# Attention, an MLP and a mixing layer in one fp32 kernel: PSUM banks of attention and of the first MLP part shared out anew, with some key parts, load steps and additions moved between queues

## The chip, the cores and the metric

The kernel runs on one core of a Trainium2 chip. The number that counts is device time in microseconds (us): the median of the runs of the whole program, launched once per run. Before the change it is 1717.0 us. A core has five engines that work side by side and meet through semaphores: TensorE (PE in the rows; PEld is its weight load), VectorE (DVE), ScalarE (ACT), GpSimd (POOL) and SyncE (SP), which here issues the DMAs. Each executes its own instructions strictly in the order in which they were written. PSUM, where PE puts its sums, has eight banks, and a bank can take a new sum only when the old one has been read out.

## What is computed

Three layers follow each other, all in fp32:

```python
def _attn_ref(q, k, v, w_phi):                     # 8 batches, 8 heads, 576 tokens, 64 wide, 128 features
    def phi(x):
        proj = np.einsum('bhsd,df->bhsf', x, w_phi)
        proj = proj - np.max(np.abs(proj), axis=-1, keepdims=True)
        return np.concatenate([np.exp(proj), np.exp(-proj)], axis=-1)
    q_p, k_p = (phi(q), phi(k))
    kv = np.einsum('bhsf,bhsd->bhfd', k_p, v)
    z = np.sum(k_p, axis=2)
    num = np.einsum('bhsf,bhfd->bhsd', q_p, kv)
    den = np.einsum('bhsf,bhf->bhs', q_p, z)[..., None] + 1e-06
    return num / den

def _moe_ref(x, g_ln, w_ch1, w_ch2):               # 512 -> 2048 -> 512
    mu, var = mean and variance of x over its last axis
    xn = (x - mu) / np.sqrt(var + 1e-06) * g_ln
    return x + np.maximum(xn @ w_ch1, 0.0) @ w_ch2

def _moe2_ref(x, w_theta, w_tok_r, w_tok_i, w_ch):
    theta = x @ w_theta
    y = mix over tokens of x * cos(theta) and x * sin(theta)
    u = x + y
    return u + np.maximum(u @ w_ch, 0.0)
```

## The kernel before

Each fp32 operand is split into a high and a low part, and a product is three matmuls (`mm3`, L72: high by high, high by low, low by high). So for every operand one engine rounds the high part and another subtracts it from the value to get the low part. `lo_vec` (L62) does that on DVE in one instruction, `lo_cut` (L68) on POOL in pieces.

**Attention** is cut into 16 units (a pair of batches by a pair of heads), each with five groups of token tiles. For the keys of a group (`Unit.keys`, L277) PE projects into a bank of `pj`, DVE takes the maximum `m` and subtracts it (`ys`), ACT does two exponentials (`pf`) and rounds the high part `kph`, and DVE makes the low part `kpl` in one instruction of 128x1024. Then PE adds keys times values into `kv` (`values`, L292). Queries (`queries`, L334) go the same way but are transposed by PE into the bank `tr` first; their low part `qp` is made on POOL. From groups 2 and 4 on, `numer` (L371) forms four numerators per batch, whose banks alternate between `nm` and `tr`, ACT copies each to `num`, and `norm` (L394) transposes `num` back. Units 0 to 4 keep their queries, and unit 0 its keys, in plain fp32 (`NATQ`, `NATK`), with no low parts.

**MLP A**, the first quarter of the MLP's 2048 hidden columns, is written into attention as filler at low priority, in 18 chunks of 256 tokens. `tokens` (L469) transposes two tiles through `ph`. Two up sums (`up`) follow, each of 256 hidden columns, in the one bank `ph`, and relu gives the parts `hh`, `hl`. The down sums (`down`) of both token tiles stay open in two banks of their own (`acc0`, `acc1`) from the first hidden block to the last, and `flush` (L505) runs the down sums of one block only after the next block's up sums. What attention leaves over is done behind it, with `wide` chunks that also use `pj`, `tr` and `nm`.

**MLP B** does the other three quarters in two rounds (`r`) over nine chunks of 512 tokens, with seven products in place of eight for each hidden block (`Hidden`, L712). `first()` makes `pa`, `pb`, `pc`; ACT copies `p1`, `u2`, `u3` out; `relu` makes the hidden parts `hb`; `second()` finishes the last two; `down` adds into four `acc` banks, one block later. `tokens_b` (L634) makes the sums `c1` to `c4` of a chunk on POOL and all high and low parts on ACT and DVE. Beside this, `advance` (L813) runs load steps that turn the 64-bit weights of later stages into fp32 parts (`raw`, `bits`, `val`, `mag`).

**The mixer** follows with its own banks.

The program text gives each instruction a priority, and a scheduler at build time chooses from it the order in which they stand on each engine. So an edit of the text moves instructions far away from it. `tc.high_priority(offset=...)` shifts the priority, and a negative offset makes filler. `tc.issue_after(ins)` puts what a block writes behind `ins` on the engine of `ins`.

Of the kernel before, what the change touches and what calls it, by code (L numbers as in the profile page):

```python
# [51 lines left out]
def body(ctx, tc, qT, kT, va, wbd, g, w1, w2, wth, wtok, wch, out):  # L52
# [78 lines left out]
    class Mlp:  # L131
# [32 lines left out]
        def down(self, f, acc, hh, hl):  # L164
            for j in range(2):
                wh, wl = self.w2[2 * f + j]
                for i in range(CT):
                    o = slice(i * P, (i + 1) * P)
                    mm3(acc[i], hh[:, j, o], hl[:, j, o], wh, wl, f == 0 and j == 0,
                        f == self.nf // 2 - 1 and j == 1)  # L170

        def relu(self, pool, ph):
# [14 lines left out]
    ps_pj, ps_tr, ps_kv, ps_nm, ps_ph, ps_ac = (pool("pj", 2), pool("tr", 1), pool("kv", 1), pool("nm", 1),  # L187
                                                pool("ph", 1), pool("ac", 1))
# [29 lines left out]
    class Unit:  # L218
        def __init__(self, u):
# [5 lines left out]
            self.final = FINAL and u == NPAIR * NHP - 1  # L225
            self.natk, self.natq = (u < NATK), (u < NATQ or u >= LASTQ)

# [49 lines left out]
        def keys(self, gi):  # L277
# [11 lines left out]
            lo_vec(kl[:, :2 * n], kp[:, :2 * n], kh[:, :2 * n])  # L289
# [44 lines left out]
        def queries(self, gi):  # L334
# [29 lines left out]
            for b, c0, o, m in parts:  # L364
                dh, dl = (t[:, :, :, c0:c0 + m].rearrange("p h s c -> p (h s) c") for t in self.qp[b])
                src = qv[:, :, o:o + m]
                hi_act(dh, src)
                lo_cut(dl, src, dh)
            return lambda: self.numer(gi)

        def numer(self, gi):  # L371
            if gi in (2, 4):
                b = 0 if gi == 2 else 1
                kh, kl = self.kv[b]
                for h in range(2):
                    for hf in range(2):
                        if hf:
                            nm = ps_tr.tile([D + 1, 288], F32, name="tr")
                        else:
                            nm = ps_nm.tile([D + 1, 288], F32, name="nm")  # L380
# [13 lines left out]
        def norm(self, t0):  # L394
            if self.alone & 1:
                xp = ps_ac.tile([P, 6, D + 1], F32, name=f"acc{t0 // 3 % 2}")
# [61 lines left out]
    def mlp_a(m):  # L458
# [44 lines left out]
        pend = None  # L503

        def flush():  # L505
            x, acc, f, hh, hl, ch = pend
            m.down(f, acc, hh, hl)
            if f == m.nf // 2 - 1:
                for i in range(CT):
                    V.tensor_tensor(x[i], acc[i], x[i], op=ALU.add)  # L510
                    SY.dma_start(out=xp_d[ch][:, i, :], in_=x[i])

        nxt = None
        for ch in range(NCH):
# [7 lines left out]
            acc = [ps_ac.tile([P, DM], F32, name=f"acc{i}") for i in range(CT)]  # L522
            for f in range(m.nf // 2):
# [5 lines left out]
                hh, hl = m.relu(p_ma, ph)  # L529
# [4 lines left out]
                if pend is not None:  # L534
                    flush()
                    yield -1
# [627 lines left out]
```

## Time and profile before

| | us |
|---|---|
| median of 3 runs | 1717.0 (1715.16 to 1718.63) |
| the profiled execution's own time | 1717.6 |
| its span, first to last instruction | 1715.8 |
| PE busy | 1655.2 (96%) |
| DVE busy | 1225.2 (71%) |
| ACT busy | 813.6 (47%) |
| POOL busy | 636.6 (37%) |
| mean granted PE clock | 0.994 |

A busy share says how long an engine had an instruction in work. Attention with its filler runs to about 586 us, the rest of MLP A to 674 us, MLP B to about 1290 us, the mixer to the end.

### The profile page before, as it was taken

The numbers are of one execution on the slowest core, as the hardware profiler recorded it, in microseconds if no ns is written. First come the engines' busy times: TensorE is split into PE (matmuls) and PEld (weight loads), VectorE is DVE, ScalarE is ACT, GpSimd is POOL, SyncE is SP. The second block draws the span as 40 slices with busy tenths as digits, with TensorE's granted clock in tenths as the row PEclk, the third lists the DMA queues.
The fourth block names the chain that finished last, engine by engine and source line by source line (L and its number), as shares of the span: only waits on it lengthen the run. The fifth ranks groups of instructions, "written<-read, shape, count | busy, mean of one in ns | idle before, by whom it ended". The sixth has DMA issues, their size and how long they took to land.

```text
span 1715.8 us, 29440 instructions
## 1 busy us (share of the span) xinstructions
PE 1655.2 (96%) x11272; PEld 1514.4 (88%) x11272; DVE 1225.2 (71%) x2306; ACT 813.6 (47%) x1672; POOL 636.6 (37%) x571
## 2 busy tenths in 40 slices
PE   7899999899999899999999999999999999999999
PEld 5687899899999798888889999988888999999999
DVE  8999887978887694778786444698866656656562
ACT  6676666656666763444453333454443223323230
POOL 6655887878876301122112111111233222322220
PEclk9999999999999999999999999999999999999999
DMA  6234333334332354255547222356660211112101
GB/s 199 72 108 119 96 116 99 96 93 133 106 101 88 127 179 160 91 187 211 192 146 271 74 74 74 119 188 219 248 226 25 77 47 53 50 47 72 53 21 42
DMA packets 107965, 201.63 MB, mean 118 GB/s; under 512 B 8369, under 2 KB 58417, under 8 KB 104497
## 3 DMA queue, kind: packets, MB, share of 16 engines
q1 hardware_dynamic: 107824, 199.76, 35.2%
q8 instruction: 89, 1.46, 0.4%
q14 instruction: 52, 0.42, 0.1%
HBM read 125.73 MB, written 69.80 MB: 114 GB/s over the span
## 4 chain that ended last, share of the span: by engine, by line
PE 81%; DVE 13%; issue 2%; ACT 2%; DMA 1%; POOL 0%; SPq 0%; DVEq 0%; POOLq 0%; ACTq 0%
PE acc L75 7%; PE acc L73 7%; PE acc L74 7%; PE mx L73 4%; PE mx L74 4%; PE mx L75 4%; PE pa L73 2%; PE pa L75 2%; PE pa L74 2%; PE ch L75 2%; PE ch L74 2%; PE ch L73 2%; PE pj L73 2%; PE pj L74 2%; PE pj L75 2%
## 5 line engine op out<-in xcount | busy, mean ns | idle before, releaser
L641 POOL TENSOR_TENSOR c<-xt 128x512 f32<-128x512 f32 x17 | 22.5, 1324 | 531.7 <-DMA xt<-xnd 468.4
L66 POOL TENSOR_TENSOR qp<-pf,qp 128x512 fp32r<-128x512 f32 (+1 forms) x132 | 159.3, 1231 | 41.5 <-ACT qp L60 41.3
L73 PE MATMUL acc<-wd,hb 128*128 128x512 f32 x432 | 170.6, 395 | 3.8 <-ACT hb L733 2.5
L73 PE MATMUL mx<-xs 128*128 128x288 f32 x576 | 171.3, 298 | 1.4 <-POOL xs L57 1.4
L74 PE MATMUL acc<-wd,hb 128*128 128x512 f32 x432 | 170.5, 395 | 0.0
L74 PE MATMUL mx<-xs 128*128 128x288 f32 x576 | 169.4, 295 | 0.0
L75 PE MATMUL mx<-xs 128*128 128x288 f32 x576 | 168.0, 295 | 0.0
L75 PE MATMUL acc<-wd,hb 128*128 128x512 f32 x432 | 154.0, 394 | 4.3 <-DVE hb L734 4.3
L63 DVE TENSOR_TENSOR kpl<-pf,kph 128x1024 fp32r<-128x1024 f32 (+1 forms) x75 | 121.2, 1616 | 10.3 <-ACT kph L60 10.3
L273 DVE TENSOR_TENSOR ys<-pj,m 128x512 f32<-128x512 f32 (+1 forms) x160 | 99.2, 628 | 27.2 <-ACT pf L283 14.9
L271 DVE TENSOR_REDUCE m<-pj 128x4 f32<-128x512 f32 (+1 forms) x160 | 98.9, 626 | 22.6 <-PE pj L75 21.7
L73 PEld LDWEIGHTS mx<-xs 128*128 128x128 f32 x576 | 108.2, 188 | 2.3 <-POOL xs L57 2.3
L74 PEld LDWEIGHTS mx<-xs 128*128 128x128 f32 x576 | 108.3, 188 | 0.1
L75 PEld LDWEIGHTS mx<-xs 128*128 128x128 f32 x576 | 107.5, 188 | 0.0
L283 ACT ACTIVATE pf<-ys 128x512 f32<-128x512 f32 (+1 forms) x160 | 85.7, 587 | 38.6 <-DVE ys L273 23.3
L73 PEld LDWEIGHTS acc<-wd,hb 128*128 128x128 f32 x432 | 81.6, 189 | 17.7 <-ACT hb L733 3.9
L74 PE MATMUL kv<-kpl,vh 128*65 128x256 f32 x300 | 86.9, 290 | 10.2 <-DVE kpl L63 9.9
L57 POOL TENSOR_SCALAR xs<-xs 128x512 fp32r<-128x512 f32 x68 | 44.0, 647 | 135.2 <-DVE xs L933 135.2
L75 PEld LDWEIGHTS acc<-wd,hb 128*128 128x128 f32 x432 | 76.6, 189 | 17.9 <-DVE hb L734 6.6
L74 PEld LDWEIGHTS acc<-wd,hb 128*128 128x128 f32 x432 | 81.8, 189 | 12.0
L60 ACT ACTIVATE u<-xT 128x288 fp32r<-128x288 f32 x64 | 28.0, 440 | 131.2 <-DVE xT L881 131.2
L73 PE MATMUL kv<-kph,vh 128*65 128x256 f32 x300 | 86.5, 288 | 1.1 <-ACT kvs L316 1.0
(333 smaller groups left out, 5761.6 us busy)
## 6 DMA issues: line engine op xcount, KB each, us to landing
xt<-xnd SPq DMA_DIRECT2D x34, 512.0 KB, 4.7
raw<-in_w SPq DMA_DIRECT2D x32, 512.0 KB, 6.0
in<-in_va SPq DMA_DIRECT2D x30, 325.0 KB, 3.1
xd<-xo SPq DMA_DIRECT2D x48, 192.0 KB, 2.2
x<-xd SPq DMA_DIRECT2D x36, 256.0 KB, 2.8
xnd<-xt SPq DMA_DIRECT2D x18, 512.0 KB, 3.1
xpd<-x SPq DMA_DIRECT2D x36, 256.0 KB, 2.2
xo<-xpd SPq DMA_DIRECT2D x18, 512.0 KB, 4.5
```

The lines of the kernel that those rows point to most:

```text
L57: G.tensor_scalar(dst, src, scale, 0.0, op0=ALU.mult, op1=ALU.add)
L60: A.activation(dst, src, AF.Copy)
L63: V.tensor_tensor(dst, src, f32(hi), op=ALU.subtract)
L66: G.tensor_tensor(dst, src, f32(hi), op=ALU.subtract)
L73: T.matmul(out_, lhsT=lh, rhs=rh, start=start, stop=False, **kw)
L74: T.matmul(out_, lhsT=lh, rhs=rl, start=False, stop=False, **kw)
L75: T.matmul(out_, lhsT=ll, rhs=rh, start=False, stop=stop, **kw)
L271: V.tensor_reduce(m[:, :2 * n], pv, axis=AX.X, op=ALU.max, apply_absolute_value=True)
L273: V.tensor_tensor(ys[:, :2 * n, :], pv, m[:, :2 * n].unsqueeze(2).to_broadcast([P, 2 * n, NF]), op=ALU.subtract)
L283: A.activation(kp[:, :2 * n, s, :], ys[:, :2 * n, :], AF.Exp, scale=sc)
L641: eng.tensor_tensor(s1, a21, a22, op=ALU.add)
```

## The change

In attention the eight banks are dealt anew: `pj` 2, `tr` 1, `kv` 1 as before, `nm` 2 in place of 1, `ph` 2 in place of 1, and the two `acc` banks are gone. All numerators take `nm`, so `tr` serves query transposes (and `wide` token transposes) alone. `ph` takes token transposes, up sums, the down sums of MLP A and the last transposes of the first four units. `down` now runs per token tile when both hidden blocks are there, and its bank is given back right after.

Further: in units 1 to 4 the `kpl` of groups 1 and 3 goes from DVE to POOL, in two pieces of 128x512. In the last unit the low query parts go from POOL to DVE. In MLP B `c22` always has its own place in place of a `raw` buffer; the order of `down` over hidden halves alternates with the token half; load steps lose their low priority and stand behind the last low part of the hidden block just written, on DVE; and the parts of chunk 1 stand behind the very first block's last high part, on ACT.

```diff
-        def down(self, f, acc, hh, hl):
-            for j in range(2):
-                wh, wl = self.w2[2 * f + j]
-                for i in range(CT):
-                    o = slice(i * P, (i + 1) * P)
-                    mm3(acc[i], hh[:, j, o], hl[:, j, o], wh, wl, f == 0 and j == 0,
-                        f == self.nf // 2 - 1 and j == 1)
+        def down(self, i, acc, hid):
+            o = slice(i * P, (i + 1) * P)
+            for f, (hh, hl) in enumerate(hid):
+                for j in range(2):
+                    wh, wl = self.w2[2 * f + j]
+                    mm3(acc, hh[:, j, o], hl[:, j, o], wh, wl, f == 0 and j == 0, f == self.nf // 2 - 1 and j == 1)
...
-    ps_pj, ps_tr, ps_kv, ps_nm, ps_ph, ps_ac = (pool("pj", 2), pool("tr", 1), pool("kv", 1), pool("nm", 1),
-                                                pool("ph", 1), pool("ac", 1))
+    ps_pj, ps_tr, ps_kv, ps_nm, ps_ph = pool("pj", 2), pool("tr", 1), pool("kv", 1), pool("nm", 2), pool("ph", 2)
...
+            self.idle = u < NATQ
...
-            lo_vec(kl[:, :2 * n], kp[:, :2 * n], kh[:, :2 * n])
+            (lo_cut if self.idle and gi in KPOOL else lo_vec)(kl[:, :2 * n], kp[:, :2 * n], kh[:, :2 * n])
...
-                lo_cut(dl, src, dh)
+                (lo_vec if self.final else lo_cut)(dl, src, dh)
...
-                        if hf:
-                            nm = ps_tr.tile([D + 1, 288], F32, name="tr")
-                        else:
-                            nm = ps_nm.tile([D + 1, 288], F32, name="nm")
+                        nm = ps_nm.tile([D + 1, 288], F32, name="nm")
...
-                xp = ps_ac.tile([P, 6, D + 1], F32, name=f"acc{t0 // 3 % 2}")
+                xp = ps_ph.tile([P, 6, D + 1], F32, name="ph")
...
-            acc = [ps_ac.tile([P, DM], F32, name=f"acc{i}") for i in range(CT)]
+            hid = []
             for f in range(m.nf // 2):
...
-                hh, hl = m.relu(p_ma, ph)
+                hid.append(m.relu(p_ma, ph))
...
-                if pend is not None:
-                    flush()
-                    yield -1
-                pend = (x, acc, f, hh, hl, ch)
-        flush()
+            for i in range(CT):
+                acc = ps_ph.tile([P, DM], F32, name="ph")
+                m.down(i, acc, hid)
+                V.tensor_tensor(x[i], acc, x[i], op=ALU.add)
+                SY.dma_start(out=xp_d[ch][:, i, :], in_=x[i])
+                yield -1
...
-            t = p_st.tile([P, NC_], F32, name="c22", tag="raw", bufs=RAWB) if pace else p_hb.tile([P, NC_], F32, name="c22")
+            t = p_hb.tile([P, NC_], F32, name="c22")
...
-            for j in range(2):
+            for n in range(2):
                 for i in range(2 * CT):
+                    j = (n + i // CT) % 2
...
-        with tc.high_priority(offset=LOWP):
-            while steps[r] < goal:
+        while steps[r] < goal:
+            with tc.issue_after(hid.low):
                 next(gl if r == 0 else gx, None)
-                steps[r] += 1
+            steps[r] += 1
...
+                if r == 0 and ch == 0 and n == 0:
+                    lead = hid.high
...
-                    cur = tokens_b(xt, G)
+                    if r == 0 and ch == 0:
+                        with tc.issue_after(lead):
+                            cur = tokens_b(xt, G)
+                    else:
+                        cur = tokens_b(xt, G)
...
+KPOOL = (1, 3)
```

Over the whole program PE has the same 11,174 instructions with the same shapes. DVE has two fewer (eight `kpl` gone, six `qp` come), POOL four more (sixteen `kpl` pieces come, twelve `qp` pieces go), ACT and the DMA queue as many as before. What moves is the order, and it is shown at three places.

**PE at the end of attention.** The names: `tr`/`nm` from `qp` are numerators, `nm` and `kv` from `num` and `kvs` are transposes back, `ph` from `xn`, `xh` are token transposes and up sums of MLP A. Before, about a unit from the end:

```order
L75 MATMUL tr_7909<-qp0_7596,kvl_7586 65x288
L403 MATMUL kv_8016<-ident_122,num_7600 128x65
L322 MATMUL nm_7781<-ident_122,kvs_7779 128x65 x4
L348 MATMUL tr_7944<-ident_122,ys_7942 128x128 x4
...
L73 MATMUL nm_7885<-qp0_7596,kvh_7585 65x288
L74 MATMUL nm_7885<-qp1_7597,kvh_7585 65x288
L75 MATMUL nm_7885<-qp0_7596,kvl_7586 65x288
```

The same numerators and the next transposes in the changed program:

```order
L75 MATMUL ph_7628<-w2_0_3_0_170,hl_7439 128x512
L73 MATMUL nm_7883<-qp0_7602,kvh_7591 65x288
...
L75 MATMUL nm_7891<-qp0_7602,kvl_7592 65x288
L488 MATMUL ph_7814<-ident_122,xn_7812 128x128 x4
L73 MATMUL nm_7899<-qp0_7602,kvh_7591 65x288
...
L488 MATMUL ph_7824<-ident_122,xn_7822 128x128 x4
L399 MATMUL nm_7915<-ident_122,num_7606 128x65 x6
...
L73 MATMUL ph_7854<-xh_7809,w1_0_0_0_162 128x256
L74 MATMUL ph_7854<-xl_7810,w1_0_0_0_162 128x256
```

Before, the last two units' numerators and transposes stand alone on PE. Now work of MLP A stands between them. Counted over the whole order, 11 of the 18 chunks had their down sums ahead of attention's last transposes before, and 9.25 have them now.

**ACT at the handover from MLP A to MLP B.** `hh` is MLP A's last relu, `s1h` to `s4h` and `a..h` are parts of MLP B's chunk 1, `p1`, `u2`, `hb` belong to chunk 0. Before:

```order
L175 ACTIVATE hh_9161<-pj_9136 128x512
L60 ACTIVATE a11h_9427<-xt_9401 128x512
L60 ACTIVATE a12h_9431<-xt_9401 128x512
L60 ACTIVATE a22h_9449<-xt_9401 128x512
L60 ACTIVATE s1h_9441<-c1_9421 128x512
L60 ACTIVATE s3h_9445<-c3_9423 128x512
L60 ACTIVATE s2h_9435<-c2_9422 128x512
L727 ACTIVATE p1_9261<-pa_9252 128x256
```

Now:

```order
L174 ACTIVATE hh_9158<-pj_9133 128x512
L714 ACTIVATE p1_9259<-pa_9250 128x256
L720 ACTIVATE hb_9249<-pb_9251 128x256
L714 ACTIVATE p1_9338<-pa_9329 128x256
...
L720 ACTIVATE hb_9249<-pc_9252 128x256
L714 ACTIVATE u2_9355<-pa_9329 128x256
L60 ACTIVATE a11h_9425<-xt_9399 128x512
L60 ACTIVATE a12h_9429<-xt_9399 128x512
```

The copy `p1` stood behind six parts of the next chunk, and now it is the first after MLP A's last relu.

**DVE in the second round of MLP B.** `hb` from `pb`, `c22`, `pa`, `pc` are the four low parts of a hidden block, `bits`, `val`, `wc` are load steps. Before, one block:

```order
L734 SCALAR_TENSOR_TENSOR hb_14130<-c22_14173,hb_14130 128x256
L115 SCALAR_TENSOR_TENSOR val_14121<-mag_14120,bits_14119 128x288
L63 TENSOR_TENSOR s2l_14349<-c2_14335,s2h_14348 128x512
L108 TENSOR_SCALAR bits_14221<-raw_14219 128x288
L734 SCALAR_TENSOR_TENSOR hb_14130<-pa_14131,hb_14130 128x256
L758 TENSOR_TENSOR pc_14133<-pc_14133,u2_14157 128x256
L63 TENSOR_TENSOR wc_14116<-val_14121,wc_14116 128x288
L109 SCALAR_TENSOR_TENSOR bits_14221<-raw_14219,bits_14221 128x288
L734 SCALAR_TENSOR_TENSOR hb_14130<-pc_14133,hb_14130 128x256
```

The same block in the changed program:

```order
L721 SCALAR_TENSOR_TENSOR hb_14128<-c22_14171,hb_14128 128x256
L115 SCALAR_TENSOR_TENSOR val_14119<-mag_14118,bits_14117 128x288
L721 SCALAR_TENSOR_TENSOR hb_14244<-pb_14246,hb_14244 128x256
L721 SCALAR_TENSOR_TENSOR hb_14128<-pa_14129,hb_14128 128x256
L745 TENSOR_TENSOR pc_14131<-pc_14131,u2_14155 128x256
L63 TENSOR_TENSOR s2l_14347<-c2_14333,s2h_14346 128x512
L63 TENSOR_TENSOR wc_14114<-val_14119,wc_14114 128x288
L721 SCALAR_TENSOR_TENSOR hb_14128<-pc_14131,hb_14128 128x256
L108 TENSOR_SCALAR bits_14219<-raw_14217 128x288
L109 SCALAR_TENSOR_TENSOR bits_14219<-raw_14217,bits_14219 128x288
```

Four load steps stood between the low parts from `c22` and from `pc`, and two do now; more of them stand in a cluster behind the last low part.

## Rows read from the trace of the kernel before

**Rows 1.** The page: span and PE's busy share.
```profile
span 1715.8 us, 29440 instructions
PE 1655.2 (96%) x11272; PEld 1514.4 (88%) x11272; DVE 1225.2 (71%) x2306; ACT 813.6 (47%) x1672; POOL 636.6 (37%) x571
```

**Rows 2.** Busy time by stretch: length, PE, PEld, DVE, ACT, POOL, granted clock, DMA.
```profile
0.00:43.00 43.00, 34.20 (x185) 25.83 (x185) 35.69 (x53) 27.65 (x53) 28.06 (x26) 0.96 0.60 198
43.00:172.00 129.00, 115.19 (x838) 96.43 (x837) 122.10 (x233) 87.22 (x178) 74.59 (x60) 0.99 0.35 100
...
343.00:553.00 210.00, 207.07 (x1610) 195.62 (x1609) 170.11 (x314) 131.56 (x247) 163.54 (x136) 1.00 0.34 104
553.00:590.00 37.00, 30.35 (x222) 26.07 (x221) 21.82 (x67) 27.84 (x53) 14.45 (x14) 0.94 0.22 68
590.00:660.00 70.00, 70.00 (x463) 64.29 (x463) 56.42 (x104) 43.89 (x80) 0.00 (x0) 0.98 0.56 192
660.00:690.00 30.00, 25.99 (x155) 23.25 (x154) 15.71 (x23) 9.51 (x20) 11.13 (x8) 0.94 0.49 163
690.00:944.00 254.00, 249.82 (x1552) 223.84 (x1551) 187.14 (x360) 114.08 (x276) 45.49 (x33) 1.00 0.51 184
...
1115.00:1262.00 147.00, 142.53 (x865) 125.58 (x863) 126.64 (x268) 71.58 (x174) 24.44 (x22) 1.00 0.65 223
```

**Rows 3.** PE's waits from 553 to 590 us: total, times, longest.
```profile
PE nm L73 <- ACT num L390: 1.2, 2, 0.7
PE tr L348 <- ACT num L390: 0.8, 3, 0.4
...
PE tr L73 <- ACT pf L362: 0.7, 1, 0.7
```

**Rows 4.** POOL's timeline near the end of attention: start, us, instruction.
```profile
577.29 2.54 POOL L66 TENSOR_TENSOR qp<-pf,qp 128x512 fp32r<-128x512 f32 x2 [2.96 <-ACT qp L60]
```

**Rows 5.** DVE's timeline at 664 us.
```profile
664.80 1.37 DVE L510 TENSOR_TENSOR x<-acc,x 128x512 f32<-128x512 f32 x2 [0.69 <-PE acc L75]
```

**Rows 6.** Timelines of ACT and of PE at the handover.
```profile
677.52 0.63 ACT L60 ACTIVATE s2h<-c 128x512 fp32r<-128x512 f32 x1 [1.14 <-POOL c L642]
678.06 0.36 ACT L727 ACTIVATE p<-pa 128x256 f32<-128x256 f32 x1
...
675.56 0.28 PE L75 MATMUL pa<-xs,wa 128*128 128x256 f32 x1
678.48 0.39 PE L73 MATMUL pa<-xs,wa 128*128 128x256 f32 x1 [2.64 <-ACT p L727]
...
682.15 0.41 PE L74 MATMUL pa<-xs,wa 128*128 128x256 f32 x1
```

**Rows 7.** Costliest DVE group, 0 to 215 us: count, busy us, mean ns.
```profile
L63 DVE TENSOR_TENSOR kpl<-pf,kph 128x1024 fp32r<-128x1024 f32 x24 | 40.9, 1703 | 1.0 <-ACT kph L60 1.0
```

**Rows 8.** Timelines of DVE and POOL early in attention.
```profile
39.18 1.21 DVE L63 TENSOR_TENSOR kpl<-pf,kph 128x1024 fp32r<-128x1024 f32 x1
...
49.44 1.80 POOL L66 TENSOR_TENSOR vl<-in,vh 128x650 fp32r<-128x650 f32 x1
49.69 2.63 DVE L63 TENSOR_TENSOR kpl<-pf,kph 128x1024 fp32r<-128x1024 f32 x1
```

**Rows 9.** PE's waits from 15 to 172 us.
```profile
PE kv L74 <- DVE kpl L63: 6.2, 5, 2.8
PE pj L73 <- DVE ys L273: 4.4, 4, 2.3
```

**Rows 10.** PE's waits from 690 to 1262 us.
```profile
PE acc L75 <- DVE hb L734: 4.3, 6, 1.5
PE acc L73 <- ACT hb L733: 1.5, 3, 0.9
```

**Rows 11.** DVE's timeline in the second round of MLP B.
```profile
1204.78 1.21 DVE L109 SCALAR_TENSOR_TENSOR bits<-raw,bits 128x288 int32<-128x288 int32 x1
1205.91 1.49 DVE L734 SCALAR_TENSOR_TENSOR hb<-c,hb 128x256 fp32r<-128x256 f32 x1
```

More of the change, by code (lines that the diff above doesn't have):

```diff
@@ L501, in tokens @@
             return x, xh, xl
[L503 to L511, printed above, removed]
         nxt = None
@@ L732, in relu @@
             h, l = self.hb[:, 0, j, o], self.hb[:, 1, j, o]
-            A.activation(h, c, AF.Relu)
-            V.scalar_tensor_tensor(l, c, 0.0, f32(h), op0=ALU.max, op1=ALU.subtract)
+            self.high = A.activation(h, c, AF.Relu).ins
+            self.low = V.scalar_tensor_tensor(l, c, 0.0, f32(h), op0=ALU.max, op1=ALU.subtract).ins
         def first(self):
@@ L761, in down @@
         def down(self, acc, start, stop):
-            for j in range(2):
+            for n in range(2):
                 for i in range(2 * CT):
+                    j = (n + i // CT) % 2
                     o = slice(i * P, (i + 1) * P)
                     mm3(acc[i], self.hb[:, 0, j, o], self.hb[:, 1, j, o], self.q.wd[:, 0, j, :],
-                        self.q.wd[:, 1, j, :], start and j == 0, stop and j == 1)
+                        self.q.wd[:, 1, j, :], start and n == 0, stop and n == 1)
     def flush_b():
@@ L802, in body @@
     gl, gx = loads_b(), loads_mix()
-    pace = True
     pend = None
@@ L1019, in body @@
                 s_st.close()
-                pace = False
                 s_xm, pm = opened(name="xm", bufs=1, side="left")
```

## Prediction

> **What bounds the kernel now.** I read the page first. PE is busy for 1655.2 of 1715.8 us [rows 1], so it is the bound, and what a change can give back is the time in which PE has nothing to do or runs at a lower clock. The change leaves PE's instructions as they are, so the whole forecast is about these gaps. Next I cut the span into stretches [rows 2]; the idle time of a stretch is its length less PE's busy time. 0 to 43 us: 8.8 us idle (the start-up is in it). 43 to 172: 13.8, and DVE is busy for 122.1 of 129 us there, so DVE sets the pace. 343 to 553: only 2.9. 553 to 590, the end of attention: 6.7, at a granted clock of 0.94. 590 to 660, the rest of MLP A: none. 660 to 690, the handover to MLP B: 4.0, at 0.94. MLP B loses 4.2 us in 690 to 944 and 4.5 in 1115 to 1262, the two stretches in which load steps run beside it. PE's list of waits and the timelines of the engines that it waits for then tell what each gap waits on.
>
> **The end of attention (gain 8, bounds 0 and 10).** PE waits here for ACT's copies of the numerators, 1.2 and 0.8 us, and for the exponentials, 0.7 [rows 3]. ACT is the engine at work (27.8 of 37 us), PE has nothing else in its order, and DVE and POOL are mostly idle [rows 2]. Stretch and clock together: 6.7 us idle, and 0.06 of 37 us = 2.2 at the lower clock, and 0.02 of 70 us = 1.4 in the stretch behind, in all 10.3. The change puts MLP A's work between the numerators (order of PE above). It moves 11 - 9.25 = 1.75 chunks to behind attention's last transposes. A chunk is 80 matmuls, and at the rate of 590 to 660 us (463 in 70 us) that is 12.1 us, so 21 us of work that PE does anyway comes later, and about as much filler now stands inside the stretch. Numerators no longer take `tr`, so a query transpose doesn't wait for a numerator's copy. The last unit's low query parts take 1.2 us on DVE (a subtraction of 128x1024 alone, first of [rows 8]) in place of 2.54 on POOL [rows 4], six times at most, and only the last of them stands on the chain. I take 8 of 10.3: the very last transposes still wait for copies.
>
> **Sharing `ph` (cost 0 to 2, in the 8 above).** What is new is that a token transpose or up sum may wait for the addition that reads a down sum out, 0.68 us each [rows 5]. I counted the cover in the new order: the matmuls between a bank's last matmul and its next use, at 0.15 us each (463 in 70 us, [rows 2]). In two places, the last steps from down sum to transpose and from transpose to up sum at the very end of attention, only four stand there, 0.6 us; everywhere else nine or more, 1.4 us. All of PE's order is queued behind such a wait, so these two cost up to 1 us each. Before, the one bank had 16 at its fewest, so no gain is due here, and 2.9 idle us of 210 in mid attention leave no room for one.
>
> **The handover (gain 3.5, bounds 0 and 5.8).** PE's matmul at 675.56 us ends a sum, and ACT copies it (`p`) only at 678.06, right behind `s2h`, which waited 1.14 us for POOL's `c`; PE waits 2.64 us [rows 6]. With `p1` first on ACT (order above) the copy can start some 0.3 us after the sum, so 2.1 us go. The idle time is followed by matmuls of 0.41 us where they are 0.28 before it [rows 6]: 256 columns at the lower of the two clock levels, granted 0.94 over the stretch, 1.8 us of 30. Three quarters of that, 1.4, should go with the wait. The parts of chunk 1 come later on ACT; PE has about 12 us of chunk 0's matmuls before it needs them, by the order, and their nine instructions of 0.63 us take under 6.
>
> **Key parts on POOL (gain 4, bounds -7 and 10.6).** In units 1 to 4 eight `kpl` leave DVE, at 1.70 us each [rows 7]: 13.6 us of an engine that is full. PE's waits that DVE ends there are 6.2 for `kpl` and 4.4 for `ys` [rows 9], the upper bound 10.6. Against it: a `kpl` takes 1.21 us alone and 2.63 when it starts 0.25 us after a POOL subtraction of 1.80 us [rows 8], so the two slow each other. The eight become sixteen pieces of 1.27 us [rows 4], 20.3 us of POOL. If each of them holds a DVE instruction up for its whole length, DVE loses 20.3 and gains 13.6: -7. But only part of DVE's work here is of the kind that is held up; `m` and `ys` read PSUM, and POOL already ran 74.6 of 129 us beside it. I take half of the piece time as lost, 10, so DVE gains some 4 net, and PE follows it.
> The Trainium skill (SBUF — State Buffer, Who interferes with whom) says that a VectorE instruction with two SBUF inputs and a GpSimd instruction that reads SBUF exclude each other: the second blocks until the first is done. By that rule the 2.63 would be 1.55 of blocking and 1.21 of work, 2.76, and the trace agrees to 0.13 us. Taken at its worst it is the -7 above and speaks against this edit.
>
> **MLP B (gain 2.5, bounds -4 and 8.7).** Idle in the two stretches with load steps: 4.2 + 4.5 = 8.7. PE waits there for DVE's `hb`, 4.3, and ACT's, 1.5 [rows 10]. An example: a load step of 1.21 us stands ahead of the low part that PE needs, which itself takes 1.49 [rows 11]. Fewer load steps stand between the low parts now, and `down` asks for the block from `c22` second and that from `pa` last, where the `pa` block came second. But the clusters behind the last low part delay the next block's addition to `pb`, and as normal work they also come earlier on ACT; at DVE's 126.6 of 147 us that can cost as much as is won on half of the blocks, hence -4. I take a quarter to a third of the 8.7. The mixer is not touched. `c22`'s own place costs nothing: it takes no instruction, and the buffer that it frees only lets loads run ahead.
>
> **Sum.** 8 + 3.5 + 4 + 2.5 = 18. The profiled execution took 1717.6 us (span 1715.8 and 1.8 around it); less 18 it is 1699.6. The median of the runs is 0.6 below it: **1699 us**.
>
> **Rivals.**
> *The filler is missed elsewhere (1707).* The 1.75 chunks that leave attention make the rest of it denser: DVE's 81% in 343 to 553 us would be some 85%, on the way to the 95% of 43 to 172, where PE idles for 10.7% of the time. If idle time rises from 1.4% to 3.4% over the 400 us up to the end, 8 us of the 18 are lost again. For it: the same work in fewer us. Against: before, 81% gave nearly no idle.
> *Key parts come late from POOL (1724, the other side).* POOL works in order, so a key part waits behind a load's subtraction (1.80, [rows 8]) and takes 2.54 in place of 1.70: 2.6 us later, eight times, 21 us, and every later matmul queues behind the `kv` matmul that waits. With the other terms' 14 that is 1717 + 21 - 14 = 1724. It decides from 14 / 8 = 1.75 us per group on. Against: `kv` comes some 6 us of PE work after its projection in both orders, and POOL has a third of its time free.
> *The waits only change places (1716).* PE is in order; where ACT is the pace at the end of attention, filler moves the wait to the next numerator, and the load clusters eat the handover's gain. Against: filler ready at the wait is exactly what PE lacked.
>
> **How the numbers follow.** Chances: the forecast 0.62 (its own range 1689 to 1706), the missed filler 0.17, the waits moving 0.08, the late key parts 0.07, and 0.06 that nearly all bounds are met (35 us at most, so under 1686). What a measurement here can tell from no change is about 0.2%, 3.4 us. The first and second and the last case are faster: 0.62 + 0.17 + 0.06 = 0.85, of which 0.01 I give to the edge; same 0.08, slower 0.08. The range 1686 to 1712 leaves out the last three cases of 0.08, 0.07 and part of 0.06.
>
> **What would show it.** Right: the stretch around the end of attention without a clock below 0.98 and under 2 us idle; no wait for `p` over 1 us at the handover; PE's waits for `kpl` in the first 172 us below 6.2 us; waits for `hb` in MLP B below 5.8. Wrong: PE waits for `kpl` ended by POOL, each over 2 us; idle time above 3% in mid attention; waits for `x` or `pb` in place of those for `hb`.

## The result and the profile after

The changed kernel takes **1699.1 us** (median of 5 runs, 1697.95 to 1708.47) where the kernel before takes 1717.0 in as many runs beside it: a ratio of 0.9903, 95% interval 0.9889 to 0.9916. (Ratios are estimated over all runs; the ratio of the two medians is 0.9896.) The forecast was 1699. A second timing, with other runs of the kernel before beside it, gave 1699.6 and a ratio of 0.9887 (0.9872 to 0.9903). The profiled execution took 1698.6 us. Its page, span and busy shares (answers to [rows 1]):

```profile
span 1696.8 us, 29401 instructions
PE 1645.5 (97%) x11272; PEld 1509.7 (89%) x11272; DVE 1195.8 (70%) x2304; ACT 815.6 (48%) x1672; POOL 648.4 (38%) x575
```

The span is 19.0 us shorter. PE's idle time, span less busy time, went from 60.6 to 51.3 us; the other 9.7 us are PE's own busy time. Four points of PE's order divide the time: the start of unit 6 (the seventh), the end of attention's last transposes, the end of MLP A's last down sum, and the mixer's first matmul (into its bank `mx`). In us from the span's start, for both kernels and for the experiments told below:

| profile of | unit 6 | last transposes | last MLP A down sum | first mixer matmul |
|---|---|---|---|---|
| before | 166.4 | 584.7 | 674.4 | 1271.2 |
| changed | 166.2 | 548.9 | 662.7 | 1252.3 |
| changed, second timing | 168.1 | 550.5 | 664.4 | 1252.9 |
| psum_only | 166.3 | 540.4 | 666.8 | 1263.3 |
| rest_only | 160.1 | 589.9 | 680.4 | 1267.9 |
| k_off | 165.9 | 541.3 | 664.9 | 1253.6 |
| lead_off | 166.5 | 550.1 | 663.9 | 1256.5 |
| b_off | 167.5 | 556.2 | 670.1 | 1262.1 |
| nmtr | 159.4 | 601.9 | 691.7 | 1279.4 |
| tr_back | 165.2 | 579.4 | 671.6 | 1261.8 |

So attention with MLP A gained 674.4 - 662.7 = 11.7 us, handover and MLP B 596.8 - 589.6 = 7.2, the mixer nothing. One profile is not exact to the microsecond. Eight of the profiles taken here (the changed kernel twice, rest_only, k_off, nmtr, tr_back, and first_after and final_off of experiments 6 and 8) have the same instructions in the same order on every engine from the handover on, and from the last down sum to the mixer they take 587.2 to 590.2 us, 588.6 in the mean. By that mean the second gain is 8.2.

Idle time is not all that a gap costs. Matmuls overlap: in attention a 128x256 matmul takes 0.28 us from start to end, but behind another one it adds only 0.12 to PE's busy time (the median of the kernel before; 0.23 for 128x512, 0.13 for 128x288). Right behind a gap it counts with its whole length. So I add these medians up, kind by kind, for all matmuls of a stretch; what the stretch takes beyond that is called lost time here, and most of it is idle time, matmuls right behind a gap, and lower clock. In us, from the same profiles:

| lost in profile of | ahead of unit 6 | units 6 to 14 | of these, unit 10 | unit 15 to the last transposes | from there to the last down sum | all |
|---|---|---|---|---|---|---|
| before | 34.9 | 22.7 | 8.2 | 9.9 | 3.6 | 71.1 |
| changed | 30.3 | 16.7 | 1.1 | 1.1 | 11.2 | 59.3 |
| changed, second timing | 32.2 | 16.5 | 1.1 | 1.0 | 11.3 | 61.0 |
| psum_only | 32.2 | 12.7 | 2.1 | 2.6 | 16.0 | 63.5 |
| rest_only | 31.5 | 25.3 | 10.0 | 15.7 | 4.4 | 76.9 |
| k_off | 31.7 | 12.7 | 2.1 | 3.7 | 13.4 | 61.5 |
| b_off | 31.5 | 23.0 | 7.3 | 1.0 | 11.3 | 66.8 |
| nmtr | 30.8 | 35.1 | 9.2 | 18.7 | 3.6 | 88.2 |
| tr_back | 36.3 | 16.8 | 1.5 | 8.9 | 6.1 | 68.1 |

The stretches that answer to [rows 2], shifted to the same work (same columns: length, PE, PEld, DVE, ACT, POOL, clock, DMA):

```profile
43.00:172.00 129.00, 119.56 (x884) 100.14 (x883) 113.94 (x233) 91.98 (x186) 96.69 (x76) 1.00 0.35 100
343.00:516.00 173.00, 168.40 (x1359) 161.55 (x1358) 143.59 (x279) 123.56 (x231) 150.81 (x124) 1.00 0.34 104
516.00:553.00 37.00, 36.68 (x272) 34.23 (x271) 25.31 (x70) 16.45 (x33) 2.57 (x2) 1.00 0.26 83
553.00:600.00 47.00, 42.39 (x271) 38.19 (x270) 45.09 (x84) 33.51 (x63) 2.93 (x2) 0.93 0.68 230
...
648.00:678.00 30.00, 28.75 (x182) 25.45 (x181) 13.35 (x25) 9.38 (x22) 5.08 (x4) 1.00 0.49 167
678.00:932.00 254.00, 247.70 (x1543) 221.91 (x1542) 190.10 (x361) 114.91 (x277) 50.52 (x36) 1.00 0.53 190
1096.00:1243.00 147.00, 145.73 (x896) 129.56 (x895) 127.70 (x273) 73.67 (x180) 23.05 (x21) 1.00 0.65 221
```

**End of attention** (516 to 553, before 553 to 590): 6.7 us idle became 0.3, the clock 0.94 became 1.00. But a new hole follows. From 553 to 600 PE idles for 4.6 us at a clock of 0.93, where 590 to 660 had no idle time and 0.98 before. PE's longest wait there, and ACT's timeline at the place:

```profile
PE ph L73 <- ACT xh L60: 2.8, 1, 2.8
```
```profile
556.20 1.15 ACT L60 ACTIVATE xs<-xs 128x512 fp32r<-128x512 f32 x2 [1.96 <-DMA xs<-xnd]
557.25 0.58 ACT L60 ACTIVATE xh<-ph 128x512 fp32r<-128x512 f32 x1
```

`xs` are parts of MLP B's first chunk, which ACT could not start before a DMA came; the part `xh` for which PE waits stands behind them.

**Handover** (648 to 678, before 660 to 690): 4.0 us idle at 0.94 became 1.25 at 1.00. ACT's timeline, answer to [rows 6]:

```profile
656.55 0.59 ACT L174 ACTIVATE hh<-pj 128x512 fp32r<-128x512 f32 x1
663.51 0.38 ACT L714 ACTIVATE p<-pa 128x256 f32<-128x256 f32 x1 [6.37 <-issue]
664.39 0.38 ACT L720 ACTIVATE hb<-pb 128x256 fp32r<-128x256 f32 x1 [0.50 <-DVE pb L730]
```

The copy `p` follows the last relu `hh`, and PE has no wait for it.

**MLP B.** Idle time in the first stretch with load steps rose from 4.2 to 6.3 us, in the second it fell from 4.5 to 1.3. PE's waits from 678 to 1243 us, against [rows 10]:

```profile
PE acc L73 <- DVE xo L767: 4.9, 4, 1.7
PE pb L73 <- DVE hb L721: 0.9, 1, 0.9
...
PE acc L73 <- ACT hb L720: 0.5, 1, 0.5
PE pa L73 <- DVE hb L721: 0.4, 1, 0.4
```

The waits for `hb`, 4.3 and 1.5 before, are 1.8 in all. New are those for `xo`, the additions that read the `acc` banks out (1.1 before; the 4.9 is the most of the eight profiles of this order, the other seven have 2.4 to 3.5). One of them, on DVE, with PE waiting for `acc` until 691.12:

```profile
685.40 1.67 DVE L110 SCALAR_TENSOR_TENSOR bits<-raw,bits 128x512 int32<-128x512 int32 x1
686.99 0.68 DVE L767 TENSOR_TENSOR xo<-acc,xo 128x512 f32<-128x512 f32 x1
687.59 1.18 DVE L115 SCALAR_TENSOR_TENSOR val<-mag,bits 128x512 f32<-128x512 f32 x1
688.69 0.68 DVE L767 TENSOR_TENSOR xo<-acc,xo 128x512 f32<-128x512 f32 x1
689.29 1.17 DVE L63 TENSOR_TENSOR a11l<-xt,a11h 128x512 fp32r<-128x512 f32 x1
690.39 1.27 DVE L767 TENSOR_TENSOR xo<-acc,xo 128x512 f32<-128x512 f32 x2
```

Load steps and a part of the next chunk now stand between the four additions.

**Key parts** (43 to 172): DVE is busy for 113.9 us where it was 122.1. The waits that answer to [rows 9], and the groups to [rows 7], 0 to 215 us (`kpl` on DVE and its pieces on POOL):

```profile
PE kv L74 <- DVE kpl L63: 2.8, 4, 1.1
PE nm L321 <- ACT kvs L315: 2.8, 4, 1.1
PE kv L74 <- POOL kpl L66: 2.3, 2, 1.4
```
```profile
L63 DVE TENSOR_TENSOR kpl<-pf,kph 128x1024 fp32r<-128x1024 f32 x17 | 25.8, 1517 | 1.3 <-ACT kph L60 1.3
L66 POOL TENSOR_TENSOR kpl<-pf,kph 128x512 fp32r<-128x512 f32 x16 | 22.1, 1400 | 2.9 <-ACT kph L60 2.9
```

### The profile page after: what moved, and what is told of

Same layout as the page of the kernel before. It is cut to its first block, busy times and chain, and to the rows that moved or that the text cites. A ratio compares the mean times of both kernels' runs of the same rounds, so it can differ in the third digit from the quotient of the medians.

```text
span 1696.8 us, 29401 instructions
## 1 busy us (share of the span) xinstructions
PE 1645.5 (97%) x11272; PEld 1509.7 (89%) x11272; DVE 1195.8 (70%) x2304; ACT 815.6 (48%) x1672; POOL 648.4 (38%) x575
## 4 chain that ended last, share of the span: by engine, by line
PE 82%; DVE 11%; issue 2%; DMA 2%; POOL 1%; ACT 1%; SPq 0%; DVEq 0%; ACTq 0%; POOLq 0%
PE acc L73 5%; PE acc L74 5%; PE acc L75 5%; PE mx L73 4%; PE mx L74 4%; PE mx L75 4%; PE ph L74 3%; PE ph L73 3%; PE ph L75 3%; PE pa L73 3%; PE pa L75 3%; PE pa L74 3%; PE ch L75 2%; PE ch L73 2%; PE ch L74 2%
## 5 line engine op out<-in xcount | busy, mean ns | idle before, releaser
L628 POOL TENSOR_TENSOR c<-xt 128x512 f32<-128x512 f32 x17 | 22.7, 1338 | 530.9 <-DMA xt<-xnd 443.5
L66 POOL TENSOR_TENSOR qp<-pf,qp 128x512 fp32r<-128x512 f32 (+1 forms) x120 | 147.7, 1255 | 5.4 <-ACT qp L60 5.4
L63 DVE TENSOR_TENSOR kpl<-pf,kph 128x1024 fp32r<-128x1024 f32 (+1 forms) x67 | 95.6, 1428 | 6.5 <-ACT kph L60 6.5
L73 PEld LDWEIGHTS acc<-wd,hb 128*128 128x128 f32 x432 | 81.7, 189 | 18.7 <-DVE xo L767 6.8
```

Source lines behind the costliest of these rows:

```text
L63: V.tensor_tensor(dst, src, f32(hi), op=ALU.subtract)
L66: G.tensor_tensor(dst, src, f32(hi), op=ALU.subtract)
L73: T.matmul(out_, lhsT=lh, rhs=rh, start=start, stop=False, **kw)
L628: eng.tensor_tensor(s1, a21, a22, op=ALU.add)
```

## The experiments

Ratios are to the kernel before on the same chip. Where a run is set against the changed kernel, it is against the second timing, 0.9887; against the first, 0.9903, it would be 2.8 us less. Such a difference of two ratios has an interval of some 4 us to either side, so that by time alone no edit undone in experiments 2, 3, 4 or 8 can be told from nothing. There the profiles have to decide. My theory was the forecast's sum: PSUM 8, handover 3.5, key parts 4, MLP B 2.5. The main rival was that the waits only change places.

**1. psum_only: the PSUM part alone.** From the changed kernel, everything else undone:

```diff
-KPOOL = (1, 3)
+KPOOL = ()
-                (lo_vec if self.final else lo_cut)(dl, src, dh)
+                lo_cut(dl, src, dh)
...
-                        with tc.issue_after(lead):
-                            cur = tokens_b(xt, G)
+                    cur = tokens_b(xt, G)
```
(and MLP B as in experiment 4)

> The kernel before with the new PSUM shares and the new down sums alone; key parts, the last unit's query parts, the parts of chunk 1 and everything in MLP B are as before. My theory: this part carries the end of attention. In the traces that stretch's loss against the time that its matmuls need went from 22.8 us to 11.9, and some 6 us come back as a stall right behind attention, so of my 8 us some 5 to 8 should show: 1709 to 1712 us, and the wait for the copy p of some 2.6 us at the handover should still be there. Rival 1, the waits only change places: within 3 us of before, 1714 to 1720. Rival 2, this part carries the whole gain and the other edits nothing: 1699 to 1703.

1709.2 us, ratio 0.9940 (0.9927 to 0.9952): 10.3 us gained, as my theory had it, and both rivals fail. Up to the last down sum the profile shows 674.4 - 666.8 = 7.6. The wait for the copy is there as before, from 652 to 682 us:

```profile
PE pa L73 <- ACT p L714: 3.3, 1, 3.3
```

**2. k_off: key parts back on DVE.** `KPOOL = ()`.

> The changed kernel with all kpl back on DVE. My theory: the edit is worth 2.4 us (the loss of the first 166 us went from 69.3 to 66.9 us in the traces) to 4 us (my term), so 1701.5 to 1703, and PE's waits for kpl ended by DVE before 172 us go from 2.8 back to some 6 us. Rival, DVE and POOL exclude each other for each piece's whole length, so the edit costs DVE as much as it saves: 1695 to 1700, with no more waits for kpl than now.

1700.9 us, ratio 0.9892 (0.9878 to 0.9905), 0.0005 above the changed kernel's second timing: 0.9 us, less than can be told. PE's waits from 15 to 172 us:

```profile
PE kv L74 <- DVE kpl L63: 6.7, 6, 2.3
PE nm L321 <- ACT kvs L315: 4.0, 6, 1.1
```

The waits for `kpl` fell by the edit as foreseen (6.7 to 2.8 + 2.3), but unit 6 starts at 165.9 us without it, and at 166.2 and 168.1 with it. The start alone says little, since 15 more matmuls stand ahead of it with the edit; but the time lost there, 31.7 us without it and 30.3 and 32.2 with it, shows at most 1 us too.

**3. lead_off: chunk 1's parts without their condition.**

```diff
-                    if r == 0 and ch == 0:
-                        with tc.issue_after(lead):
-                            cur = tokens_b(xt, G)
-                    else:
-                        cur = tokens_b(xt, G)
+                    cur = tokens_b(xt, G)
```

> The changed kernel without the condition that the parts of chunk 1 stand behind the first block's last high part. My theory: the copy p stands behind these parts on ACT again, PE waits 2 to 3 us for it and then runs at the lower clock for a few us: 3.5 to 4.8 us more, 1702.5 to 1704. Rival, MLP A's new down sums alone have already moved the handover (its last sums end in another order): 1698 to 1700 and no wait for p over 1 us.

1703.3 us, ratio 0.9905 (0.9889 to 0.9921), 0.0018 or 3.1 us above the changed kernel; last down sum to mixer takes 592.6 us, 4.0 more than the mean of 588.6 and 2.4 more than the longest of the eight. PE's waits from 650 to 690, ACT at the longer of them, and the stretches:

```profile
PE pb L73 <- DVE hb L721: 4.2, 1, 4.2
PE pa L73 <- ACT p L714: 2.2, 1, 2.2
```
```profile
675.59 0.67 ACT L107 ACTIVATE mag<-raw 128x512 f32<-128x512 f32 x1 [6.00 <-DMA raw<-in_w]
```
```profile
650.00:680.00 30.00, 22.38 (x134) 19.63 (x133) 14.11 (x19) 8.20 (x17) 11.63 (x8) 0.95 0.56 193
680.00:934.00 254.00, 252.25 (x1571) 226.74 (x1571) 187.74 (x364) 117.66 (x280) 44.15 (x32) 1.00 0.52 187
```

At the handover 30 - 22.4 = 7.6 us are idle, 6.4 more than in the changed kernel. But in the first stretch of MLP B only 1.75 are, where the changed kernel has 6.3: with the parts early, DVE is not late for `xo` there (waits of 1.2 us in place of 4.9). So the condition wins 6.4 us of idle time and some at the lower clock, and 4 to 5 are paid again. The copy `p` is only the smaller part of the win: PE waits 2.2 us for it, as my theory had it, but 4.2 for a low part `hb`, because ACT stands still for 6.0 us ahead of a load step (`mag`) whose weights are still in a DMA, and the high part stands behind that step. The forecast did not have this wait.

**4. b_off: MLP B as before.**

```diff
-        while steps[r] < goal:
-            with tc.issue_after(hid.low):
-                next(gl if r == 0 else gx, None)
-            steps[r] += 1
+        with tc.high_priority(offset=LOWP):
+            while steps[r] < goal:
+                next(gl if r == 0 else gx, None)
+                steps[r] += 1
...
-                    j = (n + i // CT) % 2
+                    j = n
```

> The changed kernel with MLP B's load steps at low priority, its down order and c22's place as before. My theory: 2.4 us more (the loss of MLP B went from 64.1 to 61.7 us in the traces), 1701.5, with waits for hb back at some 5.8 us. Rival, the load steps behind the low parts pay as much at the additions that read out acc (PE's wait for xo went from 1.1 to 4.9 us) as they win at hb: 1697 to 1700, with the waits for xo under 2 us.

1702.9 us, ratio 0.9900 (0.9885 to 0.9915): 0.0013 or 2.2 us above the changed kernel. Last down sum to mixer takes 592.0 us, 3.4 more than the mean of the eight and 1.8 more than their longest. The waits for `hb` are back in part (2.4, 1.0 and 0.8 us, where I had foreseen 5.8), and those for `xo` are 0.9, under 2 as the rival had it. The length of the stretch speaks for my theory.

**5. nmtr and tr_back: numerators on `tr` again.** tr_back is the first edit alone; nmtr has the second as well:

```diff
-                        nm = ps_nm.tile([D + 1, 288], F32, name="nm")
+                        nm = (ps_tr if hf else ps_nm).tile([D + 1, 288], F32, name="tr" if hf else "nm")
```
```diff
-pool("nm", 2), pool("ph", 2)
+pool("nm", 1), pool("ph", 3)
```

> The changed kernel with the numerators back on nm and tr in turn, one bank nm, and the bank that this frees given to ph (three). Theory A, the gain at the end of attention comes from the filler of MLP A that now stands there, for which ph's banks count and the numerators' own banks do not: within 2 us of the changed kernel, and no stretch in the last 75 us of attention with a clock under 0.98. Theory B, it comes from numerators that no longer hold tr against query transposes: 4 to 8 us slower, with waits of tr for num of some 1 to 2 us at the end of attention as in the kernel before.

> The changed kernel with one thing undone: every second numerator takes the bank tr again, beside the two banks nm; ph keeps its two banks. Theory, what counts is that tr is free for query transposes: as slow as the run with one nm and three ph, 1720 to 1735 us, with eleven chunks of MLP A ahead of attention's end in the order and the loss spread over attention's whole second half. Rival, what counts is a second bank nm (numerators, transposes back and the kvs transposes share it): within 5 us of the changed kernel, 1698 to 1705.

nmtr: 1731.7 us, ratio 1.0073 (1.0053 to 1.0092), 32 us slower than the changed kernel beside it (1699.6) and slower than before. tr_back: 1704.9 us, ratio 0.9915 (0.9898 to 0.9933), 4.8 us slower by the second timing, 2.1 by the first. So both of my theories on nmtr were too small, and the rival on tr_back holds: releasing `tr` is worth some 5 us at most. The rest, about 27, is the step from tr_back to nmtr, a bank taken from `nm` and given to `ph`. That the loss is `nm`'s is argued: no run changes `nm` without `ph`, and the order moves with both. In both orders eleven chunks stand ahead of attention's end, as before the change; the 9.25 of the changed kernel come from taking the numerators off `tr`. PE at the end of attention in nmtr, where one bank `nm` serves numerators, transposes back (`ident,num`) and the transposes of `kvs`:

```profile
584.73 0.56 PE L399 MATMUL nm<-ident,num 65*128 65x65 f32 x6 [1.22 <-DVE xo L405]
...
590.38 0.50 PE L73 MATMUL nm<-qp,kvh 128*65 128x288 f32 x1 [1.38 <-DVE kvl L63]
596.84 0.32 PE L73 MATMUL nm<-qp,kvh 128*65 128x288 f32 x1 [1.17 <-DVE xo L405]
598.30 0.34 PE L73 MATMUL nm<-qp,kvh 128*65 128x288 f32 x1 [0.50 <-ACT num L386]
```

Each takes the bank only when its last content is read out.

**6. first_after, wide0: the hole behind attention.** Chunk 0's parts stand behind a relu of MLP A; wide0 sets `WIDE = 0` as well.

```diff
-            cur = tokens_b(xt, V, [*(first[:, i] for i in range(4, 7)), s4, *hls])
+            with tc.issue_after(ma.high):
+                cur = tokens_b(xt, V, [*(first[:, i] for i in range(4, 7)), s4, *hls])
```
(`ma.high` is the last relu written)

> The changed kernel, with the parts of MLP B's chunk 0 put behind a relu of MLP A on ACT, so that the high part xh of the first transposes behind attention does not stand behind parts that wait for a DMA. Theory: PE's wait for xh of 2.8 us at 558 us goes, and most of the lower clock behind it (0.92 in 551 to 594 us): 3 to 5 us faster than the changed kernel. Rival: the next wait, for xl and xn from DVE, which is full there, ends only 1 us sooner: at most 1.5 us faster.

> The run with chunk 0's parts behind a relu, and the first chunk behind attention is already a wide one (its transposes take nm and tr, xn comes from ACT, its second up sum takes pj, the next chunk's transposes stand ahead of its end). Theory: behind attention the two ph banks are what the restart lacks, so its loss (14 us against the matmuls' own time in 554 to 601 us, where the rest of MLP A has some 8%, 3 us) shrinks by 4 to 8 us: 1690 to 1695 us. Rival: DVE and ACT work through attention's last read-outs there whatever the banks are: within 2 us of the run before, 1696 to 1700.

first_after: 1697.9 us, ratio 0.9874 (0.9856 to 0.9892), no difference that can be told from the changed kernel's 0.9887. wide0: 1700.8 us, 0.9890 (0.9875 to 0.9906). The theories fail, and in time the rivals hold (wide0 lies 0.8 us outside its rival's range). In first_after the wait for `xh` is down to 0.7 us, and 1.9 for `xn` has come. In wide0 PE and ACT show what is behind it:

```profile
561.29 1.12 PE L488 MATMUL nm<-ident,xn 128*128 128x128 f32 x4 [6.93 <-ACT xn L482]
```
```profile
560.42 0.81 ACT L482 ACTIVATE xn<-x,lnb,lrs 128x512 f32<-128x512 f32 x1 [11.36 <-DMA x<-xd]
```

The next chunk's tokens are still in a DMA. The trace shows the load late in the queue on SP, which works in order:

```profile
554.35 1.08 SPq L473 DMA_DIRECT2D x<-xd  x2
```

It stands behind attention's last two stores (`xd` from `xo`, issued at 547.99 and 551.24 us, after SP had waited for DVE) and two loads of `xs`, and lands at 560.33, 6.0 us after its issue. So the hole may hang on where these loads stand on SP; no run moves them.

**7. best1: first_after, and the parts of the next chunk behind the read-out of `acc`.**

```diff
+                        with ExitStack() as behind:
+                            for ins in read:
+                                behind.enter_context(tc.issue_after(ins))
                             cur = tokens_b(xt, G)
```
(`read` holds the four additions to `xo`)

> As the run before, and in MLP B the parts of the next chunk stand behind the additions that read out acc, on DVE. Theory: of PE's 4.9 us of waits for xo the ones behind a low part a11l (1.06 of 1.41 and 1.06 us there, two of four) go, so 1 to 2.5 us beyond the run before. Rival: the parts come later and PE waits for them in place of xo: no difference or 1 us slower than the run before.

1698.7 us, ratio 0.9883 (0.9867 to 0.9899). The waits for `xo` are gone, and 3.0 us for `hb` from `pb` have come: the rival (0.0009 above first_after).

**8. final_off: the last unit's low query parts on POOL again** (`lo_cut(dl, src, dh)`).

> The changed kernel with the last unit's low query parts on POOL again, in pieces. Theory: they stand on the chain only once, at 1.3 us more (2.54 in place of 1.2), so 1 to 3 us slower, 1700 to 1703. Rival: filler covers them in the new order, so no difference, 1698 to 1700.

1699.0 us, ratio 0.9876 (0.9855 to 0.9897): no difference, the rival.

**9. rest_only: the change without its PSUM part**, the kernel before with the edits of 2, 3, 4 and 8.

> The kernel before with all of the change but its PSUM part: banks, numerators, down sums of MLP A and last transposes of the first units are as before; key parts on POOL, the last unit's low query parts, the parts of chunk 1 and everything in MLP B are as changed. Theory, the two halves add up: PSUM alone was 9.8 us faster and the whole 19.2 (against the kernel before on the same chip), so this one is 8 to 11 us faster: 1708 to 1711 where the kernel before takes 1719, with PE's wait for p at the handover under 1 us. Rival, the small edits only pay on the new banks' order, as each one that was undone alone cost at most 4 us: 1712 to 1719, with the waits at the end of attention and at the handover as before.

1715.6 us, ratio 0.9983 (0.9974 to 0.9992): only 3 us gained, where the terms were 10. The rival holds as to the time, but not at the handover: from the last down sum to the mixer this kernel takes 587.5 us, 9.3 less than before, and PE waits for no `p`. What it loses, it loses in attention. Unit 6 starts 6.3 us sooner than before, of which some 3 are matmuls that stand behind this point now (967 ahead of it, 989 before) and 3.4 less lost time; attention ends 5.2 us later. Two places show it, a wait at 324 us and the end of attention:

```profile
PE kv L74 <- DVE kpl L63: 5.4, 1, 5.4
```
```profile
558.00:595.00 37.00, 29.20 (x184) 24.48 (x183) 23.67 (x68) 22.55 (x42) 1.71 (x2) 0.80 0.17 52
```

## Why the prediction came out right, and where it did not

**The sum** was right, 18 us forecast and 17.9 measured (16.7 by the ratio). But its largest term came from another place than the one forecast, one term came to almost nothing, and two came out larger. So there was luck in the 1699.

**PSUM, 8 us.** The size came out: 10.3 (8.3 to 12.5) alone by time, 7.6 by the profile. The place did not. The step on the stretch itself was right: its clock is 1.00 and under 2 us are idle, and with the clock it gained 6.4 + 2.2 = 8.6 of the 8.9 us that 553 to 590 offered. But "the very last transposes still wait" put the remaining loss in the wrong place. It lies behind attention: 4.6 us idle and 0.07 of 47 = 3.3 at the lower clock, 7.9, against 1.4 before, so 6.5 go back. From the last transposes to the last down sum it takes 113.8 us where it took 89.7, 24.1 more: 101 more matmuls of MLP A stand there, which by their medians are 16.5 us (the forecast had 21), and 7.6 more are lost. From unit 15 to the last down sum, lost time fell only from 13.5 to 12.3 us, and in psum_only it rose to 18.6. So the step that was wrong is that filler in the stretch is won for good: the restart behind attention takes most of it back.

What carried the term instead lies in attention ahead of its end. Units 6 to 14 lost 22.7 us before, 16.7 in the changed kernel and 12.7 in psum_only, and most of the change is unit 10 (8.2 and 1.1). The stretch around it, before and after:

```profile
314.00:402.00 88.00, 82.58 (x631) 77.53 (x632) 71.61 (x130) 54.87 (x103) 68.61 (x59) 0.98 0.35 107
```
```profile
306.00:375.00 69.00, 68.16 (x548) 65.31 (x546) 56.54 (x105) 49.86 (x93) 63.62 (x52) 1.00 0.39 111
```

The forecast saw no gain in mid attention because only 2.9 us were idle from 343 to 553 us. For that stretch it was right (lost time 7.0, and 7.0 in 343 to 516 now). But its list of stretches leaves out 172 to 343 us, where 9.2 us were idle; now it is 6.5, with 50 more matmuls done. Idle time also hides a part: from unit 6 to the last transposes it fell from 19.2 to 11.4 us, but busy time fell by 27.8 for 129 matmuls fewer, which by their medians are 20.9. Of the 6.9 that remain, 5.0 are matmuls right behind a gap, of which there were 41 and are 19.

Which bank counts the table shows across runs. With one bank `nm` (before, rest_only, nmtr) PE has 41, 36 and 62 gaps from unit 6 to the last transposes, and unit 10 loses 8.2 to 10.0 us; with two (all other profiles) it has 17 to 30 gaps, and unit 10 loses 1.1 to 2.1, but for b_off, where one slow `kpl` costs 6 (last section). So a second `nm` goes with the gain; I had put the gain on filler and on `tr`. What is lost in unit 10 stands on DVE: the ten small steps of a normalization (128x9 values) come there with one `nm`, among the `kpl` and `ys` that PE needs, and take 6.8 to 8.3 us together; with two they are over before unit 10 starts and take 1.7 to 4.4. PE waits there for `kpl`, 2.3 us before and 5.4 in rest_only. One step, before and after:

```profile
326.80 1.23 DVE L210 SCALAR_TENSOR_TENSOR ltm<-ltm,lrs 128x9 f32<-128x9 f32 x1
```
```profile
299.71 0.15 DVE L207 TENSOR_TENSOR ltm<-lrs,lve 128x9 f32<-128x9 f32 x1
```

So the bank seems to act by the order that it leads to; no run moves these steps alone.

**Sharing `ph`, 0 to 2.** No cost shows: in the changed kernel no wait of PE at `ph` is ended by the addition that reads a down sum out.

**Handover, 3.5 us, and MLP B, 2.5 us.** Both came out somewhat larger. Four kernels give all combinations, from the last down sum to the mixer: with neither edit 596.4 us (psum_only), with the condition on chunk 1 alone 592.0 (b_off), with MLP B's edits alone 592.6 (lead_off), with both 588.6 (mean of eight). So the condition is worth 4.0 to 4.4, MLP B's edits 3.4 to 3.8, and here they nearly add up: 7.8 in place of 6.0. By time they are 3.1 and 2.2, each with some 4 us to either side. At the handover the wait for `p` and the clock went as described (2.75 us idle and 1.8 of clock). What the forecast had only as a rival's half sentence, and among its signs of being wrong, is the new wait for `xo`: 2.4 to 4.9 us in the eight profiles with both edits, 1.2 and 0.9 with one. It is one loss that the two edits make together.

**Key parts, 4 us.** Too much: 0.9, not told from nothing. DVE was relieved, by more than I took (8.2 us in 43 to 172 in place of 4), and the waits for `kpl` are shorter. The step that failed is "PE follows it": PE then waits for POOL's pieces (1.40 us each, and not 1.27) and for ACT. The late key parts of the rival did not come; POOL ended two waits, the longest 1.4 us.

**The rivals.** The missed filler came in part: in 343 to 516 us 2.7% of the time is idle where 1.4% was, and DVE is busy for 83% in place of 81%; the sign of being wrong was 3%. The waits changed places in part, to the restart behind attention and to `xo`. One reading was wrong without weight in the sum: at the end of attention DVE was not mostly idle, [rows 2] have it busy for 21.8 of 37 us.

**The rest.** In attention the parts do not add up. Alone, PSUM gains 10.3 and all else 2.9, together 13.2, where the whole gains 16.7 to 19.4; with the lower of these the intervals still overlap. But all else alone (rest_only) gains 9.3 from the last down sum on and is 6.0 later at that point: it wins 3.4 of lost time ahead of unit 6 and gives back more in units 6 to 15, where no edit of it but the last unit's query parts changes an instruction: its edits move the order there. In the changed kernel the same edits cost attention nothing. With the old banks the single `nm` is a likely cause, argued from the gaps above and not shown for this kernel. My sum took for granted that a part is worth the same in any order.

## What to carry to other kernels

Count the kinds of sums that each PSUM bank serves before counting idle time, and give a second bank to the kind on the chain, rather than to the filler: here one bank for numerators and two kinds of transposes went with 36 to 62 gaps of PE, two with 17 to 30. List every stretch, also those with little idle time, and charge filler that is moved with the restart at the place where it ends. An edit that relieves a busy engine is worth only what the next engine in the chain leaves over; here 8 us of DVE time gave 0.9 us, which can't be told from nothing. Where work is put behind a condition to clear one queue, look at which read-out it then stands ahead of.

## What the runs showed of the hardware

The same subtraction can take three times as long from one run to the next. In attention b_off and the changed kernel have the same instructions in the same order on each engine, yet at one place `kpl` took 6.56 us on DVE in the first and 2.31 in the second timing of the other. (Seven profiles with the same order up to there have 2.29 to 2.32; the long one came once.) DVE and then POOL in b_off:

```profile
306.47 6.56 DVE L63 TENSOR_TENSOR kpl<-pf,kph 128x1024 fp32r<-128x1024 f32 x1
```
```profile
306.09 1.60 POOL L66 TENSOR_TENSOR vl<-in,vh 128x650 fp32r<-128x650 f32 x1
307.64 1.28 POOL L66 TENSOR_TENSOR kl<-in,kh 128x512 fp32r<-128x512 f32 x1
308.88 2.49 POOL L66 TENSOR_TENSOR qp<-pf,qp 128x512 fp32r<-128x512 f32 x2
311.35 0.61 POOL L57 TENSOR_SCALAR qh<-in 128x512 fp32r<-128x512 f32 x1
```

And in the changed kernel's second timing:

```profile
306.88 2.31 DVE L63 TENSOR_TENSOR kpl<-pf,kph 128x1024 fp32r<-128x1024 f32 x1
```
```profile
306.51 1.59 POOL L66 TENSOR_TENSOR vl<-in,vh 128x650 fp32r<-128x650 f32 x1
308.06 2.28 POOL L66 TENSOR_TENSOR kl<-in,kh 128x512 fp32r<-128x512 f32 x1
```

In the second, `kpl` waits for `vl` only, and then POOL's `kl` takes 1 us longer: it waits in its turn. In the first, four subtractions of POOL pass in a row before `kpl` can end. PE waited 5.13 us for it, and attention ended 5.7 us later. The Trainium skill (SBUF — State Buffer, Who interferes with whom) says that issue order decides which of the two blocks the other. The trace agrees that they block each other, but here the blocked one was passed over three times, by instructions that started after it.

Small instructions pay the same price. A step of 128x9 values for the normalization (`ltm`) takes 0.17 us alone on DVE and took 1.25 at 555.15 us, beside a POOL addition of 1.26 at 555.12. The spread of a kernel's runs, 10.5 us for the changed one in its first timing, may come from such races; no run here shows how much of it does.
